# A two-level Strassen-Winograd channel product on one core: second pass in groups of 1024 tokens, with all weights read from DRAM

## The chip, the cores and the metric

The kernel runs on one core of one Trainium2 chip. The metric is device time in microseconds of one execution, measured on the core. Smaller is better. Everything is fp32.

## What is computed

An attention block without softmax is followed by an MLP mixer. B = 8 batches, 8 heads of 64, S = 576 tokens, 512 channels.

```python
kv = np.einsum('bhsd,bhse->bhde', k, v)
out = np.einsum('bhsd,bhde->bhse', q, kv)
rms = np.sqrt(np.mean(out * out, axis=-1, keepdims=True) + 1e-06)
x = (out / rms * g_norm)                 # then heads are put side by side: (B, S, 512)
h = np.maximum(x.transpose(0, 2, 1) @ w_tok1, 0.0) @ w_tok2      # 576 -> 256 -> 576
u = x + h.transpose(0, 2, 1)
h2 = np.maximum(u @ w_ch1, 0.0) @ w_ch2                          # 512 -> 1536 -> 512
return u + h2
```

The change concerns the last two lines, the channel product over all 8 x 576 = 4608 tokens.

## The kernel before

The **first pass** computes attention and the token mixing for pairs of batches, and writes u to DRAM (`u_dram`). It ends at about 197 us of the profiled execution and is not touched.

The tokens are cut into nine units of 512: unit b (0 to 7) holds the first 512 tokens of batch b, unit 8 the 64 last ones of all batches. **Group 0** (unit 0) is computed by `channel1_once` and `channel2_once` with one level of Strassen-Winograd, seven products of half-size matrices in place of eight. Meanwhile the weights for the second pass are prepared: `mix_ch1`, `mix_ch2` make the sums of the outer level, `split` those of the inner level.

The **second pass** computes groups 1 to 8, one unit each, with two levels: `channel1` (u times w_ch1) and `channel2` (times w_ch2) each have seven outer blocks (`ORDER1`, `ORDER2`), and each block has seven inner products of three matmuls with 128 moving columns, both levels numbered 1 to 7. The inner level of one block is the function `outer`. A block starts every seven *places*; `PLACE` says at which place after the start of its block each inner product stands, so that neighbouring blocks interleave. `put(place, step)` hangs other steps (evictions of PSUM, sums on VectorE, transfers) behind the product of a place. At the end of the program one loop walks through the places and emits the product and then the steps; every engine and queue gets its work in this order.

The inner products of a block share PSUM tiles: a takes products 1, 6, 7 and 4 in turn and is read after each; c gets a copy of product 1 and product 2 on top; b takes 5 and 3. Tiles a and b come from a ring of six (`m_psum`), c from a ring of two. Where a block has a `base` (blocks 2, 5 and 4 of channel1, block 6 of channel2) the reads are adds on VectorE, else copies on ScalarE. `write` joins a PSUM tile with what was read before (u2, u3).

Of the seven weight parts of a block, four lie in SBUF (`w_ch1`, `w_ch2`, the outer sums in `late["w2"]`, `d2`); the three inner sums are stored by `split` to DRAM (`sums_dram`) and fetched by `fetch_sums` three blocks ahead. All of `split` runs on VectorE with three buffers (`sv`).

The activations come to `uT`, transposed, by a way of their own: `fetch_t` loads a tile of u, `turn_blocks` transposes 32x32 blocks on VectorE and stores them to DRAM, `fetch_u` reads them in the order wanted. `outer_u` and `inner_u` fill the 7x7 outer and inner sums of `uT`. In channel2 the steps `ins[o]` make the inner sums of the hidden activations, A and S1 to S4 their outer sums, `xadd` and `radd` add the finished blocks to the residual `xg`, and `store` writes the result. Some sums of channel1 run on GpSimd.

All transfers here are issued on SyncE's queue (SP), except the stores of u_dram (GpSimd) and some at the very end (ScalarE).

Of the kernel before, what the change touches and what calls it, by code (L numbers as in the profile page):

```python
# [20 lines left out]
def kernel(  # L21
# [49 lines left out]
    NG = B + 1  # L71
# [8 lines left out]
    consts = pool("consts", 1)  # L80
# [19 lines left out]
    w_ch1 = consts.tile([P, 4, 4, FQ], F32, name="w_ch1")  # L100
    w_ch2 = consts.tile([P, 4, NS, DH], F32, name="w_ch2")
# [3 lines left out]
    u_dram = [dram.tile([J * P, DM], F32, name=f"u_dram{g}") for g in range(NG)]  # L105
# [126 lines left out]
    IN = {1: {5: 0, 6: 1, 3: 2}, 2: {5: 0, 6: 1, 4: 2}}  # L232

    def part(weight, o, n, sums=None):

        if n in IN[weight]:
            t = sums[:, IN[weight][n]]
            return t if weight == 1 else t.rearrange("p (w e) -> p w e", w=W)
        if weight == 1:
            return (w_ch1[:, SA[o]] if SA[o] < 4 else late["w2"][:, SA[o] - 4])[:, SA[n]]  # L240
        return w2_of(o)[:, ts(int(n in (2, 3)), W), ts(int(n in (7, 3)), P)]
# [34 lines left out]
    def w2_of(n):  # L276
# [3 lines left out]
    sums_dram = {(w, o): dram.tile([P, 3, FQ], F32, name=f"sums{w}{o}")  # L280
                 for w in (1, 2) for o in SA}

    def sums_tile():
        return late["sums"].tile([P, 3, FQ], F32, name="sums", tag="sums")

    def split(weight, o):


        at = []
        steps = (s_sums if weight == 1 else t_sums)(lambda n: part(weight, o, n, at[0]))  # L290

        def first():
            at.append(late["sv"].tile([P, 3, FQ], F32, name="sv"))
            steps[0]()

        def last():
            steps[3]()
            dma(sums_dram[weight, o], at[0])

        return [first, steps[1], last], steps[2]  # L300
# [244 lines left out]

    def fetch_x(g, i):

        if g < NG:
            if i == 0:
                xg[g] = late["xg"].tile([P, J, DM], F32, name="xg")  # L550
            dma(xg[g][:, ts(i, 2)], u_dram[g].rearrange("(t p) e -> p t e", p=P)[:, ts(i, 2)])

    def fetch_t(g, i):

        if g < NG:
            xt[g, i] = late["xt" if g else "xt0"].tile([P, DM], F32, name="xt")
            dma(xt[g, i], u_dram[g][ts(i, P)])

# [4 lines left out]
    def turn_blocks(g, i):  # L565
        if g >= NG:
            return
        half, n = i // 2, 2 * (i % 2)
        if n == 0:
            blocks[g] = late["y" if g else "y0"].tile([P, NC, 2, NC, Q], F32, name="y")  # L570
        for o in range(2):
            keep(nc.vector.transpose(
                blocks[g][:, :, o, n:n + 2].rearrange("p b n t -> p n b t"),
                xt[g, i][:, ts(o, DH)].rearrange("p (n b t) -> p n b t", n=2, b=NC)))
        if n:
            t = blocks_dram[g, half] = dram.tile([NC, Q, NC, 2 * P], F32, name=f"blocks{g}{half}")
            for a in range(NC):
                dma(t[:, :, a].rearrange("b i x -> i b x"),
                    blocks[g][ds(a * Q, Q)].rearrange("p b o n t -> p b (o n t)"))

    def fetch_u(g, half):

        if g >= NG:
            return
        if half == 0:
            uT[g] = late["u"].tile([P, 7, NC, 7, Q], F32, name="uT")
        for o in range(2):
            dma(uT[g][:, 2 * half + o, :, :4].rearrange("p a n t -> p a (n t)"),
                blocks_dram[g, half].rearrange("b i a x -> (b i) a x")[:, :, ts(o, P)])

    def outer_u(g):

        return t_sums(lambda n: uT[g][:, SB[n], :, :4]) if g < NG else []

    def inner_u(g, lo, hi):

        return t_sums(lambda n: uT[g][:, lo:hi, :, SB[n]]) if g < NG else []
# [6 lines left out]
    def v_tile(g, i):  # L604

        if (g, i) not in V:
            V[g, i] = late["v"].tile([P, NS, 2, P], F32, name=f"v{i}")
        return V[g, i]
# [11 lines left out]
    def r_tile():  # L620
        return late["r"].tile([P, 2, DH], F32, name="r", tag="r")

    def channel1_once(g):
# [4 lines left out]
        def pair(d):  # L628
# [15 lines left out]
            def first():  # L644
                for n in ("t1", "u2", "u3"):
                    at[n] = r_tile().rearrange("p i (j t) -> p i j t", j=2)
                for n in (1, 6, 7, 5):
                    at[f"p{n}"] = m_psum(shape, f"ps_v{n}")
                product(1, at["p1"], True, False)
                copy(at["t1"], at["p1"])  # L650
# [34 lines left out]
    def channel2_once(g):  # L685
# [16 lines left out]
        t1, u2, u3 = (r_tile() for _ in range(3))  # L702
# [24 lines left out]
        def fourth():  # L727
            product(4, p7, False, True)
            tensor_add(quarter(1, 0), p7, quarter(1, 0))
            store(g, xg, 1)  # L730

        def third():
            product(3, p5, False, True)
            tensor_add(quarter(0, 1), p5, quarter(0, 1))
            store(g, xg, 0)
# [6 lines left out]
    PLACE = {1: 0, 2: 8, 6: 3, 5: 4, 7: 6, 4: 9, 3: 12}  # L742
# [5 lines left out]
    def outer(place, size, mul, to, base=None, act=copy, onto=False):  # L748

        banks, t = {}, {}

        def product(n, name, start, stop):
            if start:
                banks[name] = m_psum([P, size], f"ps_{name}")
            mul(n, banks[name], start, stop)

        def temp(n, bufs):
            t[n] = late["tmp"].tile([P, FQ], F32, name=n, tag=n, bufs=bufs)[:, :size]
            t[n] = fit(t[n])
            return t[n]

        def fit(flat):
            return flat if size == P else flat.rearrange("p (w t) -> p w t", w=W)

        def read(o, i, j):

            if base:
                tensor_add(o, fit(banks["a"]), base(i, j))
            else:
                copy(o, fit(banks["a"]))

        def read_first():
            banks["c"] = late["c"].tile([P, DM], F32, name="ps_c", tag="c")[:, :size]
            read(fit(banks["c"]), 0, 0)

        def write(i, j, name, n):  # L780
            tensor_add(to(i, j), fit(banks[name]), to(i, j) if onto else t[n])

        def put_on(i, j, n):
            if onto:
                tensor_add(to(i, j), to(i, j), t[n])

        def take(i, j, name, act):
            if onto:
                tensor_add(to(i, j), banks[name], to(i, j))
            else:  # L790
                act(to(i, j), fit(banks[name]))

        def at(n, name, start, stop, *steps):
            def all_of():
                product(n, name, start, stop)
                for step in steps:
                    step()

            products[place + PLACE[n]] = all_of

        at(1, "a", True, False, read_first)
        at(6, "a", False, False, lambda: read(temp("u2", 2), 0, 1))
        at(5, "b", True, False)
        at(7, "a", False, False, lambda: read(temp("u3", 1), 1, 1))
        at(2, "c", False, True, lambda: take(0, 0, "c", act))
        put(place + PLACE[7] + (1 if onto else 2), do(put_on, 1, 1, "u3"), do(write, 1, 1, "b", "u3"))
        at(4, "a", False, True, lambda: take(1, 0, "a", copy) if onto else read(to(1, 0), 1, 0))
        put(place + PLACE[4], do(put_on, 0, 1, "u2"))
        at(3, "b", False, True)
        put(place + PLACE[3] + 1, do(write, 0, 1, "b", "u2"))  # L810

# [12 lines left out]
    sums, v_in_parts = {}, {}  # L824

    def fetch_sums(n):
        if n < len(order):
            w, _, o = order[n]
            sums[n] = sums_tile()
            dma(sums[n], sums_dram[w, o])  # L830

# [3 lines left out]
    def channel1(g, n0):  # L837
# [4 lines left out]
        def first(i, o):  # L842
            n = n0 + i

            def mul(p, ps, start, stop):
                for w in range(W):
                    matmul(ps[:, ts(w, P)], lhsT=part(1, o, p, sums[n])[:, ts(w, P)],
                           rhs=uT[g][:, SB[o], :, SB[p]], start=(start and w == 0), stop=stop,
# [3 lines left out]
            outer(7 * n, FQ, mul, lambda i, j: sub(v_tile(g, TO[o]), i, j),  # L852
                  base and (lambda i, j: sub(v_tile(g, base), i, j)), relu if o in (2, 4) else copy)
            put(7 * n + PLACE[3] + 1, do(fetch_sums, n + 3))

        for i, o in enumerate(ORDER1):
            first(i, o)

# [8 lines left out]
        for place, step in zip((21, 22), add(3, 3, 1)):  # L867
            put(b + place, step)
        for place, i, j in ((30, 0, 0), (31, 1, 1), (32, 1, 0), (35, 0, 1)):
            put(b + place, do(lambda i, j: tensor_add(*(sub(v_tile(g, t), i, j) for t in (1, 4, 3)),  # L870
                                                      engine=nc.gpsimd), i, j))
        put(b + 43, *add(7, 5, 4, nc.gpsimd))

        for t, *places in ((2, None, 29, 28, 25), (7, 47, 47, 48, 48), (1, None, 50, 46, 47)):
# [4 lines left out]
        for place, f, i in ((18, turn_blocks, 0), (19, fetch_t, 1), (29, turn_blocks, 1), (30, fetch_t, 2),  # L879
                            (40, turn_blocks, 2), (41, fetch_t, 3), (49, turn_blocks, 3), (70, fetch_t, 4)):  # L880
            put(b + place, do(f, g + 1 + i // J, i % J))
        if g > 1:
            steps = outer_u(g)[1:]
            for place, step in zip((0, 0, 2, 3, 4, 5, 7, 9), steps + [inner_u(g, 1, 2)[2]] + inner_u(g, 2, 7)):
                put(b + place, step)

    def channel2(g, n0):
# [3 lines left out]
        def second(i, o):  # L891
# [3 lines left out]
            def mul(p, ps, start, stop):  # L895
                v = v_in_parts[g, o](p)
                w = part(2, o, p, sums[n])
                for s in range(W):
# [357 lines left out]
```

## Time and profile before

| what | value |
|---|---|
| median of three runs | 806.33 us (806.32 to 810.31) |
| the profiled execution | 805.97 us |
| its span, first to last instruction | 803.9 us |
| first pass ends, group 0 begins (TensorE) | 196.8 us |
| channel2_once begins | 233.7 us |
| first product of the second pass | 264.7 us |
| one group of the second pass | 65.8 us |
| last matmul ends | 798.7 us |

The span is what the profile covers; 2.1 us of the execution lie outside it. A matmul's end is modelled in the profile, so durations of single matmuls overlap, and the rate is read from one start to the next. The stage boundaries are starts of the first matmul on the tiles ps_v, ps_w and ps_a in TensorE's timeline. These are the transfers that the change has to do with, with their number, size and the median time from issue to landing:

```profile
sums<-sums SPq DMA_DIRECT2D x112, 576.0 KB, 4.1
...
xt<-u_dram SPq DMA_DIRECT2D x36, 256.0 KB, 4.1
blocks<-y SPq DMA_DIRECT2D x72, 128.0 KB, 2.6
uT<-blocks SPq DMA_DIRECT2D x36, 256.0 KB, 4.8
...
sums<-sv SPq DMA_DIRECT2D x14, 576.0 KB, 2.8
```

### The profile page before, as it was taken

How to read it: one execution, taken by the hardware profiler on the slowest of the kernel's cores; microseconds unless marked ns; L12 is line 12 of the kernel's file. 1: busy time of each engine (PE TensorE's matmuls, PEld its weight loads, DVE VectorE, ACT ScalarE, POOL GpSimd, SP SyncE). 2: the span in 40 equal slices, each digit the busy share in tenths (PEclk: the TensorE clock that was granted, in tenths of full speed). 3: DMA queues.
4: the chain of work that ended last, by engine and by line, in shares of the span. 5: the costliest groups of instructions: out<-in, count | busy, mean ns of one | idle time of the engine just before them, and what ended most of it. 6: DMA issues, size and time to landing. Idle time of an engine off the chain costs nothing.

```text
span 803.9 us, 17541 instructions
## 1 busy us (share of the span) xinstructions
PE 784.7 (98%) x7008; PEld 692.2 (86%) x7008; DVE 645.0 (80%) x1265; ACT 294.3 (37%) x761; POOL 91.3 (11%) x93
## 2 busy tenths in 40 slices
PE   5999999999999999999999999999999999999997
PEld 5655545535888999999999999999999999999997
DVE  2666576796896978978987987997897899799687
ACT  2356564845210224234244234333423423423331
POOL 1211111111000021011003003001101200300300
PEclk9999999999999999999999999999999999999999
DMA  9999998457258477378468648738736845864642
GB/s 291 310 337 333 350 360 297 158 188 243 102 182 287 176 229 231 129 221 269 155 194 249 198 148 259 220 117 274 254 123 221 262 160 189 245 199 134 208 148 82
DMA packets 95040, 175.49 MB, mean 218 GB/s; under 512 B 7024, under 2 KB 54128, under 8 KB 94960
## 3 DMA queue, kind: packets, MB, share of 16 engines
q1 hardware_dynamic: 90656, 163.21, 63.3%
q0 software_dynamic: 2624, 9.44, 3.0%
q10 hardware_dynamic: 1680, 1.74, 0.7%
q8 instruction: 55, 0.90, 0.4%
q14 instruction: 25, 0.20, 0.1%
HBM read 137.79 MB, written 36.57 MB: 217 GB/s over the span
## 4 chain that ended last, share of the span: by engine, by line
PE 89%; DMA 4%; DVE 3%; ACT 2%; issue 1%; SPq 0%; ACTq 0%; DVEq 0%
PE ps_a L128 37%; PE ps_b L128 19%; PE ps_c L128 10%; PE ps_h L128 8%; PE ps_u L128 7%; PE ps_v L128 3%; PE ps_kv L128 2%; DMA v_in<-in_v_dram 2%; PE ps_w L128 2%; PE ps_o L128 2%; ACT x L453 1%; DMA k_in<-in_k_dram 1%; DMA sums<-sums 1%; DVE uT L119 1%; DVE sv L119 1%
## 5 line engine op out<-in xcount | busy, mean ns | idle before, releaser
L119 POOL TENSOR_TENSOR v<-v,v 128x384 f32<-128x384 f32 (+1 forms) x48 | 61.4, 1300 | 504.4 <-ACT v L125 464.6
L125 ACT COPY u<-ps_a 128x128 f32<-128x128 f32 (+1 forms) x160 | 56.1, 351 | 157.8 <-PE ps_a L128 155.7
L128 PE MATMUL ps_b<-uT,sums 128*128 128x128 f32 x672 | 86.3, 276 | 0.2 <-DVE v L119 0.2
L128 PEld LDWEIGHTS ps_b<-uT,sums 128*128 128x128 f32 x672 | 80.7, 192 | 0.5 <-DVE v L119 0.4
L119 DVE TENSOR_TENSOR v<-v,v 128x768 f32<-128x768 f32 (+1 forms) x86 | 79.4, 931 | 1.5 <-ACT r L125 0.5
L128 PE MATMUL ps_a<-uT,w_ch 128*128 128x128 f32 x576 | 78.8, 275 | 0.0
L125 ACT COPY ps_c<-ps_a 128x128 f32<-128x128 f32 (+1 forms) x80 | 26.9, 336 | 129.6 <-PE ps_a L128 97.9
L119 DVE TENSOR_TENSOR v<-ps_b,u 128x384 f32<-128x384 f32 x112 | 61.4, 548 | 13.7 <-PE ps_b L128 12.0
L128 PEld LDWEIGHTS ps_a<-uT,w_ch 128*128 128x128 f32 x576 | 71.5, 192 | 0.1
L128 PE MATMUL ps_u<-h,w_tok 128*128 128x512 f32 (+1 forms) x160 | 67.3, 607 | 0.2
L128 PE MATMUL ps_h<-x,w_tok 128*128 128x512 f32 (+1 forms) x160 | 65.4, 603 | 0.0
L119 DVE TENSOR_TENSOR uT<-uT 128x512 f32<-128x512 f32 (+4 forms) x103 | 63.0, 628 | 0.8
L128 PE MATMUL ps_a<-uT,w 128*128 128x128 f32 x432 | 60.0, 275 | 0.0
L128 PEld LDWEIGHTS ps_a<-uT,w 128*128 128x128 f32 x432 | 54.0, 192 | 0.0
L128 PEld LDWEIGHTS ps_h<-x,w_tok 128*128 128x128 f32 (+1 forms) x160 | 26.1, 189 | 31.9 <-issue 27.7
L128 PEld LDWEIGHTS ps_u<-h,w_tok 128*128 128x128 f32 (+1 forms) x160 | 24.7, 179 | 31.2 <-issue 25.4
L119 DVE TENSOR_TENSOR xg<-xg,r 128x512 f32<-128x512 f32 x74 | 49.9, 684 | 0.7
L119 DVE TENSOR_TENSOR sv<-v 128x384 f32<-128x384 f32 x80 | 43.3, 550 | 8.8 <-ACT v L122 8.8
L122 ACT ACTIVATE v<-v 128x384 f32<-128x384 f32 (+1 forms) x86 | 42.5, 528 | 21.4 <-DVE v L119 20.9
L399 DVE TENSOR_TENSOR x<-ps_o,g_sb 128x512 f32<-128x512 f32 x32 | 21.5, 686 | 34.6 <-PE ps_o L128 30.0
L128 PE MATMUL ps_a<-uT,sums 128*128 128x128 f32 x336 | 46.9, 276 | 1.2 <-DMA sums<-sums 1.0
L128 PE MATMUL ps_a<-sums,sv 128*128 128x128 f32 x336 | 47.0, 276 | 0.0
(131 smaller groups left out, 1560.1 us busy)
## 6 DMA issues: line engine op xcount, KB each, us to landing
sums<-sums SPq DMA_DIRECT2D x112, 576.0 KB, 4.1
qT<-in_q_dram SPq DMA_DIRECT2D x8, 1152.0 KB, 9.1
xt<-u_dram SPq DMA_DIRECT2D x36, 256.0 KB, 4.1
blocks<-y SPq DMA_DIRECT2D x72, 128.0 KB, 2.6
uT<-blocks SPq DMA_DIRECT2D x36, 256.0 KB, 4.8
xg<-u_dram SPq DMA_DIRECT2D x18, 512.0 KB, 5.3
k_in<-in_k_dram SPq DMA_DIRECT2D x16, 512.0 KB, 9.0
u_dram<-x POOLq DMA_DIRECT2D x16, 512.0 KB, 6.3
```

What stands on the lines that cost most here:

```text
L119: keep(engine.tensor_tensor(out=o, in0=a, in1=b, op=op))
L122: keep(nc.scalar.activation(o, a, AF.Relu))
L125: keep(nc.scalar.copy(o, a))
L128: keep(nc.tensor.matmul(*a, **kw))
L399: keep(nc.vector.tensor_mul(x, bank[c, h], g_sb.to_broadcast([P, number(c), D])))
L453: keep(nc.scalar.activation(x[:, k, h], x[:, k, h], AF.Copy, scale=inv[:, k, h]))
```

## The change

Groups 1 to 4 of the second pass now hold two units each (`units`), so 1024 tokens. channel1's matmuls have 256 moving columns (T), and there are half as many of them. In channel2 the moving side is the weights, 128 columns as before; its matmuls are as many as before, two row tiles to a product. Sums, evictions and residual adds are half as many and twice as long.

None of the weights stays in SBUF after group 0. `split` stores all seven parts of a block to DRAM: three (of the block itself) as they are, two sums made on VectorE and two on GpSimd. It has two buffers for w_ch1 (during channel1_once) and one for w_ch2 (`svb`, during channel2_once and the first twelve places). `fetch_w` reads the parts in four pieces, into two buffers each, at 12, 9, 7 and 4 places before their block.

PSUM is cut anew: a and b have one tile of two banks each, d has two. a takes products 1 and 2; d gets a copy of product 1 and then 6, 7 and 4; b takes 5 and 3. The places within a block change with it. The last block of all has an order of its own (`LAST`).

The inner sums of the activations are no longer kept for all of `uT`; `inner_u` makes four for each block, two buffers ahead, and the outer sums lie in a ring of three (`us`). The transposition of the two units of the next group is spread over channel1. In the change-over from group 0, unit 2 is transposed and fetched during channel2_once.

```diff
-    NG = B + 1
+    NU = B + 1
+    NG = 1 + B // 2
+    T = 2 * P
...
+        def first():
+            at.append(late["sv0"].tile([P, 4, FQ], F32, name="sv0"))
+            for n in (1, 2, 4 if weight == 1 else 3):
+                dma(wide(to[:, POS[n]]), of(n))
+            if weight == 1:
+                tensor_add(own(5), of(7), of(4))
+            else:
+                tensor_add(own(5), of(7), of(1), ALU.subtract)
+
+        def second():
+            tensor_add(own(6), own(5), of(1), ALU.subtract) if weight == 1 else tensor_add(
+                own(6), of(3), own(5), ALU.subtract)
+
+        def third():
+            tensor_add(own(7), of(1 if weight == 1 else 3), of(7), ALU.subtract, nc.gpsimd)
+
+        def fourth():
+            tensor_add(own(3 if weight == 1 else 4), of(2), own(6), ALU.subtract, nc.gpsimd)
...
+                dma(to[:, 1:3], t[:, :2])
+                dma(to[:, 5:], t[:, 2:])
...
-    PLACE = {1: 0, 2: 8, 6: 3, 5: 4, 7: 6, 4: 9, 3: 12}
+    PLACE = {1: 0, 5: 1, 6: 3, 2: 4, 3: 5, 7: 6, 4: 9}
+    LAST = {1: 0, 5: 1, 6: 3, 2: 4, 7: 5, 3: 6, 4: 7}
...
+        def first():
+            bank("a")
+            mul(1, banks["a"], True, False)
+            bank("d")
+            copy(banks["d"], banks["a"])
+
+        def fifth():
+            bank("b")
+            mul(5, banks["b"], True, False)
+            read(temp("p5", 2), "b", 1, 1)
...
+        def sixth():
+            mul(6, banks["d"], False, False)
+            read(temp("u2", 1), "d", 0, 1)
...
+        def join(i, j, name, n):
+            tensor_add(to(i, j), fit(banks[name]), to(i, j) if onto else fit(t[n]))
...
+        put(place + places[3], do(join, 0, 1, "b", "u2"))
+        put(place + places[7], do(join, 1, 1, "d", "p5"))
...
+    def fetch_ahead(n):
+        for k, place in enumerate((-12, -9, -7, -4)):
+            if 7 * n + place >= 0:
+                put(7 * n + place, do(fetch_w, n, k))
...
             def mul(p, ps, start, stop):
+                wt, u = w_part(n, p), u_part(g, o, p)
                 for w in range(W):
-                    matmul(ps[:, ts(w, P)], lhsT=part(1, o, p, sums[n])[:, ts(w, P)],
-                           rhs=uT[g][:, SB[o], :, SB[p]], start=(start and w == 0), stop=stop,
+                    matmul(ps[:, ts(w, T)], lhsT=wt[:, ts(w, P)],
+                           rhs=u.rearrange("p a n t -> p n a t"), start=(start and w != 1), stop=stop,
...
+            for place, step in zip((-4, -2, 2, 5), inner_u(g, o)):
...
-        for place, step in zip((21, 22), add(3, 3, 1)):
+        for place, step in zip((15, 18), add(3, 3, 1)):
...
+        for k, place in enumerate((12, 17, 23, 27, 33, 37, 42, 46)):
+            u = units(g + 1)[k // J]
+            put(b + place, do(turn_blocks, u, k % J))
...
+        for place, step in zip((-2, 1, 10, 18), outer_u(g)):
...
+    late["sv0"] = pool("svb", 1, "right", w2s)
+    fill, turns = lasts + parts2[:20], turn_unit(2)
+    for i, f in enumerate(turns):
+        fill.insert(3 * i, f)
...
+    fill += [do(fetch_u, 1, 1, 0), do(fetch_u, 1, 1, 1), do(fetch_w, 1, 1)] + inner_u(1, 1)[:2] + outer_u(1)[:1]
+    weave(channel2_once(0), fill)
+    banks.close()
+    for n, size in (("a", 1), ("b", 1), ("d", 2)):
+        late[n] = pool(n, size, space=bass.MemoryType.PSUM)
...
+    for n, f in enumerate(parts2[20:]):
+        put(2 + 3 * n // 2, f)
```

## The prediction

> **What bounds the kernel now.** I read the page first, then TensorE's waits, the stretches of the second pass, and the order of time on single engines. TensorE has work almost throughout, and the chain of work that ended last is made of it:
>
> ```profile
> span 803.9 us, 17541 instructions
> PE 784.7 (98%) x7008; PEld 692.2 (86%) x7008; DVE 645.0 (80%) x1265; ACT 294.3 (37%) x761; POOL 91.3 (11%) x93
> ...
> PE 89%; DMA 4%; DVE 3%; ACT 2%; issue 1%; SPq 0%; ACTq 0%; DVEq 0%
> ```
>
> The waits of TensorE, longest first, are small, and only these lie in the part that changes:
>
> ```profile
> PE ps_a L128 <- DMA sums<-sums: 1.0, 1, 1.0
> ...
> PE ps_a L128 <- ACT ps_c L125: 0.2, 1, 0.2
> ...
> PE ps_b L128 <- DVE v L119: 0.2, 1, 0.2
> ```
>
> So TensorE's own rate and new waits are what count. Its rate is read from starts in the timeline, since ends are modelled:
>
> ```profile
> 209.49 1.89 PE L128 MATMUL ps_v<-uT,w_ch 128*128 128x256 f32 x8
> 211.21 1.89 PE L128 MATMUL ps_v<-uT,w 128*128 128x256 f32 x8
> 212.94 1.89 PE L128 MATMUL ps_v<-uT,w_ch 128*128 128x256 f32 x8
> ```
> ```profile
> 277.42 0.83 PE L128 MATMUL ps_a<-uT,w 128*128 128x128 f32 x6
> 278.09 0.83 PE L128 MATMUL ps_a<-uT,w_ch 128*128 128x128 f32 x6
> 278.76 0.83 PE L128 MATMUL ps_c<-uT,w 128*128 128x128 f32 x6
> ```
>
> An fp32 matmul leaves two records. Eight records of 256 columns take 1.727 us, so one matmul 432 ns; six of 128 columns take 0.670 us, so one 223.4 ns. Two narrow ones (446.8) against one wide one save 15.0 ns. Next, how full VectorE is. The columns are length, then busy time (and count) of TensorE, weight load, VectorE, ScalarE, GpSimd, then clock, DMA share, GB/s; the first line is one group of 512 tokens, the second a busy stretch of the first-group code:
>
> ```profile
> 303.60:369.40 65.80, 65.80 (x590) 65.78 (x590) 56.87 (x117) 22.86 (x65) 7.68 (x6) 1.00 0.65 207
> 245.00:255.00 10.00, 10.00 (x48) 8.81 (x47) 6.22 (x12) 0.00 (x0) 0.00 (x0) 1.00 1.06 379
> ```
>
> VectorE is at 86% and stalls nobody. Back to back it takes less than its mean duration, 0.465 us for 384 elements where the group's mean is 0.55:
>
> ```profile
> 275.09 0.55 DVE L119 TENSOR_TENSOR v<-ps_b,u 128x384 f32<-128x384 f32 x1
> 275.56 0.55 DVE L119 TENSOR_TENSOR w_ch<-w_ch 128x384 f32<-128x384 f32 x1
> 276.02 0.55 DVE L119 TENSOR_TENSOR d<-d 128x384 f32<-128x384 f32 x1
> ```
>
> The same 0.08 taken off other means gives steps of 0.34 (256 elements), 0.60 (512), 0.87 (768), 1.68 (1536).
>
> [...]
>
> **The change, part by part.**
>
> *Wide products.* channel1 has 7x7x3 = 147 matmuls for each of 8 groups, 1176; they become 588. 588 x 15.0 ns = 8.8 us less on the path. channel2 keeps 128 columns and the same number of matmuls. A place of the order takes 3 x 0.432 = 1.30 us in channel1 and 6 x 0.2234 = 1.34 in channel2 (before: 0.67).
>
> *VectorE in total.* A group of 1024 tokens has, in channel1: 14 joins and 12 adds of 768 (22.6), 28 `inner_u` of 256 (9.4), 4 `outer_u` of 1024 (4.6), 2 adds of 1536 (3.4), 8 pairs of transposes of 0.76 (6.1) = 46; in channel2: 28 sums of 768 (24.4), 10 of 1536 (16.8), 10 of 1024 (11.4), 18 of 256 (6.0) = 59. 105 of 129 us is 81%, less than the 86% now. VectorE doesn't become the bound on average.
>
> *PSUM in groups.* Before, b lay in a ring of six and a join could be late by several products. Now a and b have one buffer each. The join of product 3 (place 5) must have read b before product 5 of the next block (place 8): two products, 2.6 us. d is equally short. So VectorE may lag by about 2.6 us, and its work is bunched. Counting lag place by place (work at the steps above, less 1.30 per place): it is level at the end of product 15; p5 (0.87) and the 1536 add (1.68) leave 2.55; place 16 (one `ui`, 0.34) leaves 1.6; place 17 (u2 0.87, `ui` 0.34, transposes 0.76) 2.3; place 18 (a read of a 0.87, the other 1536 add 1.68, `outer_u` 1.14) 4.7; the join of place 19 is finished at 4.7 - 1.3 + 0.87 = 4.2 us after its product, against 2.6: late by 1.6, the join of d behind it by 1.9 in all. At places 37 to 41, where `ins[1]` adds four sums of 0.87 to the reads of block 4, the same count gives 1.3. That is 3.2 a group, 1.6 in the last (no transposes): 11 us. Bounds: 0, if VectorE is ahead when it arrives, and 16, if waits between dependent adds (0.58 instead of 0.47 in the timeline) are added. The same count for the kernel before gives a largest lag of 1.8, which its ring of six absorbs. I take 9.
>
> *Weights from DRAM.* Seven parts of each of the 14 blocks are stored, 14 x 7 x 196.6 KB = 19.3 MB where 8.3 were. Read: 4 x 19.3 = 77 MB against 66. Each fetch stands 12 places, 16 us, ahead of its use, and lands in 4.1 (row of sums). Steady traffic is near 30 MB in 129 us, 230 GB/s: hidden. A part that is late costs directly; I take nothing, at most 0.5 us a block (28 in all).
>
> *Change-over.* Here the cover goes. In channel2_once (7 products of 5.18 us, 36.3) five `split(2, o)` are woven in, with one buffer `svb`. Each first add on VectorE waits for the stores of the split before it. One round: two adds 1.0, two GpSimd adds 2 x 1.0 (its 128x384 row), issue 0.3, landing 2.8 (row sums<-sv), 6.1 at least; with four transposed-block stores (0.43 each to issue) ahead on SP and VectorE's other work I get starts at 13, 22, 30, 37.5 and 44 us. VectorE takes its work in order, so behind the waiting fifth split stand the last read of PSUM (0.6) and the two first `ui` sums that place 1 needs (46 us, where TensorE is ready at 37.6). And `fetch_u` of unit 2 stands on SP behind the last store of that split, which waits for two GpSimd adds, and behind `store(0, 0)`, which waits for VectorE: issued at 48 us, four of them, landed at 53 (4.8 by the row uT<-blocks), then two `outer_u` sums of 1.14, one add of a split and `ui` 7: 56. TensorE would reach the product that needs it (place 6) at 36.3 + 5 x 1.30 = 42.8. Wait 13.3 us, part of it already at place 1. Bounds: 4 (rounds of 5.7, from 13) and 22 (traffic here is 14 MB, at 379 GB/s 38 us, more than the 36.3 available, and landing then takes the 9 of the loads of k_in). The trace of before loses 1.2 at this spot (the 1.0 and 0.2), which goes. In channel1_once the splits have two buffers and GpSimd takes half; one more transposition ahead of the first reads of PSUM: +1.
>
> *End.* In the last block seven products stand in eight places without a gap to work off the sums: VectorE has 10.6 us behind place 43 where TensorE has 8; I get its last add 3 us after TensorE's ideal end, 0.9 now. Stores similar. +2.5 (1 to 4).
>
> Sum: 803.9 - 8.8 + 9 + 13.3 - 1.2 + 1 + 2.5 = 819.7 of span. Outside the span lie 805.97 - 803.9 = 2.1; the median of the runs is 0.4 above the profiled execution. 822.
>
> **Rivals.** (1) Only the change-over costs, since TensorE's own pauses put VectorE ahead: 822 - 9 = 813. For it: 81% against 86%; against it: the single b. (2) The other side: landing in the change-over is fast enough that place 6 is met within about 4 us, and VectorE stalls are below 1 and the end costs 1: 803.9 - 8.8 - 1.2 + 4 + 1 + 1 + 2.1 = 802. It decides when a split round is below 5.7 us. [...] (3) Weights arrive late: 0.5 us a block, 822 + 28 = 850, if SP is held up by waits for VectorE (its longest now are 12.6 and 19.2 us); against it: 16 us of lead.
>
> **How the numbers follow.** Forecast 0.50 (own range 814 to 830), rival 1 0.17, rival 2 0.26, of which half is faster and half within 0.5%, rival 3 0.07. A difference under 0.5% (4 us) can't be told from none. Faster 0.13, same 0.15, slower 0.72. Range 802 to 834.
>
> **What would show it.** Right: 128x256 matmuls at 432 ns; a pause of TensorE of 10 us or more, in pieces, just after channel2_once with VectorE or uT as releaser; in each group short waits of ps_b or ps_d for VectorE near a third and four fifths of channel1. Wrong: no gap at the change-over, or waits for w parts.

## The result and the profile after

The changed kernel takes 868.49 us (median of four runs, 866.68 to 869.07), the kernel before 806.33; the ratio is 1.0755, with a 95% interval of 1.0724 to 1.0787. The profiled execution of the changed kernel has a span of 864.9 us where the one before had 803.9, so 61.0 us are to be explained. The direction was forecast, the size was not: 822 us, with a range up to 834.

These lines of the page of the changed kernel answer to the first ones shown of before:

```profile
span 864.9 us, 14846 instructions
PE 793.9 (92%) x5832; PEld 656.8 (76%) x5832; DVE 641.7 (74%) x890; ACT 265.3 (31%) x513; POOL 118.6 (14%) x97
...
PE 50%; DVE 16%; DMA 7%; issue 3%; SPq 2%; POOL 1%; ACT 0%; DVEq 0%; POOLq 0%; ACTq 0%
```

TensorE's share of the chain that ended last fell from 89% to 50%, VectorE's rose from 3% to 16%, although VectorE is busy for a smaller share of the span than before (74% against 80%). That is the pattern of an engine that has capacity but is late at certain places. TensorE's waits say which (engine, tile and line; releaser; sum, times, longest one):

```profile
PE ps_d L131 <- DVE v L122: 13.9, 9, 2.6
PE ps_b L131 <- DVE ui L122: 12.0, 1, 12.0
PE ps_d L131 <- DVE u L122: 9.0, 4, 2.5
...
PE ps_b L131 <- DVE v L122: 6.2, 6, 1.7
PE ps_b L131 <- DVE sv L122: 3.9, 4, 1.0
...
PE ps_d L131 <- DVE ui L122: 3.0, 1, 3.0
...
PE ps_d L131 <- DVE xg L122: 2.7, 1, 2.7
```

The two with `ui` are the change-over, once each. The others with `v`, `u` and `sv` come back in each of the four groups, and `xg` is the end. No wait of TensorE for a weight `w` stands in this list. Nor does anything wait for GpSimd's sums in channel1: in the list of the waits of all engines GpSimd is the releaser once, for 0.2 us, in the first pass, and the queue SP waits for it only ahead of stores of `sv`, the sums of the splits. So it is not the slowness of these sums themselves that delays the work behind them.

The change-over in TensorE's timeline (start, duration; the bracket is idle time before the instruction and its releaser):

```profile
270.10 1.46 PE L131 MATMUL ps_a<-uT,w 128*128 128x256 f32 x6
283.58 2.93 PE L131 MATMUL ps_b<-ui,w 128*128 128x256 f32 x6 [12.03 <-DVE ui L122]
286.30 2.76 PE L131 MATMUL ps_d<-ui,w 128*128 128x256 f32 x6
288.86 1.85 PE L131 MATMUL ps_a<-uT,w 128*128 128x256 f32 x6
290.55 1.46 PE L131 MATMUL ps_b<-uT,w 128*128 128x256 f32 x6
295.04 1.32 PE L131 MATMUL ps_d<-ui,w 128*128 128x256 f32 x5 [3.03 <-DVE ui L122]
```

Starts are 1.30 us apart when TensorE runs freely. After the pause of 12.03 us two steps of 2.72 and 2.56 us follow: TensorE came back at half its clock (0.50 from 283.6 to 288.8 us). The table of stretches (columns as before: length, busy time of TensorE, weight load, VectorE, ScalarE and GpSimd, then clock, DMA share, GB/s) shows how full the DMA engines are while channel2_once runs, in the kernel before (first line) and in the changed one (second line); its last line shows the slow clock of the changed kernel:

```profile
234.00:270.00 36.00, 36.00 (x172) 31.76 (x171) 29.39 (x48) 0.59 (x1) 0.00 (x0) 1.00 0.63 223
...
234.00:270.00 36.00, 36.00 (x168) 31.69 (x168) 21.25 (x35) 1.22 (x2) 9.14 (x8) 1.00 0.97 309
...
283.60:288.80 5.20, 5.20 (x12) 4.13 (x13) 0.38 (x1) 0.80 (x1) 0.58 (x1) 0.50 1.01 332
```

What the forecast did not have at all is seen when the timelines of GpSimd and VectorE in group 2 are laid side by side:

```profile
471.70 1.82 POOL L122 TENSOR_TENSOR v<-v,v 128x768 f32<-128x768 f32 x1 [1.23 <-DVE v L122]
...
478.26 3.47 POOL L122 TENSOR_TENSOR v<-v,v 128x1536 f32<-128x1536 f32 x1 [2.30 <-DVE v L122]
487.04 3.54 POOL L122 TENSOR_TENSOR v<-v,v 128x1536 f32<-128x1536 f32 x1 [5.31 <-DVE v L122]
...
472.23 0.91 DVE L122 TENSOR_TENSOR p<-ps_b,v 128x768 f32<-128x768 f32 x1
...
478.03 3.98 DVE L122 TENSOR_TENSOR ui<-us,ui 128x256 f32<-128x256 f32 x2
...
486.88 0.41 DVE L122 TENSOR_TENSOR ui<-us 128x256 f32<-128x256 f32 x1
...
487.90 3.51 DVE L122 TENSOR_TENSOR sv<-v 128x768 f32<-128x768 f32 x1
```

An add on VectorE of 256 elements takes 0.41 us (at 486.88, begun just before GpSimd's sum at 487.04). Two of them take 3.98 us at 478.03, while GpSimd adds 1536 elements: the first began before GpSimd and took 0.42 us, the second ended 0.3 us after GpSimd. At 487.90 an add of 768 elements takes 3.51 us beside another GpSimd sum. At 472.23 an add of 768 elements with one input in PSUM takes its usual 0.91 beside a GpSimd sum. All overlaps from 268 us on say the same. Of 30 VectorE adds with both inputs in SBUF that began while GpSimd was adding, 29 were drawn out (the other one began 0.07 us before GpSimd's end). Of 13 that began before GpSimd none was, and of 15 adds with an input in PSUM none was. The rows by shape (count, busy time, mean ns) give the sum of it; the first three are VectorE's, the last two GpSimd's:

```profile
L122 DVE TENSOR_TENSOR sv<-v 128x768 f32<-128x768 f32 x40 | 48.6, 1222 | 0.0
L122 DVE TENSOR_TENSOR ui<-us,ui 128x256 f32<-128x256 f32 x24 | 29.0, 1222 | 0.0
L122 DVE TENSOR_TENSOR sv<-v,sv 128x768 f32<-128x768 f32 x28 | 26.6, 949 | 0.0
...
L122 POOL TENSOR_TENSOR v<-v,v 128x768 f32<-128x768 f32 x16 | 29.6, 1861 | 381.6 <-ACT v L128 376.7 <-DVE v L122 4.9
L122 POOL TENSOR_TENSOR v<-v,v 128x1536 f32<-128x1536 f32 x8 | 28.1, 3509 | 27.3 <-DVE v L122 27.3
```

Two adds of the same size, `sv<-v` and `sv<-v,sv`, have the same mean when undisturbed (948 and 951 ns in e1_memset below); here the first has 1222 ns, the second 949. `ui<-us,ui` has 1222 ns where an undisturbed one has some 416.

A ledger of the 61.0 us. A pause is the time from one start of TensorE to the next above the ideal step (1.295 or 1.340 us a product), steps of over 0.12 us only:

| stage | before | after |
|---|---|---|
| pauses in the change-over (waits 12.03 and 3.03, the slow clock 3.1) | 1.5 | 18.5 |
| pauses in the four groups (eight before) | 0.3 | 46.8 |
| pause at the end | none | 2.9 |
| start of the last product to the end of the span | 6.0 | 9.4 |
| wide products in place of narrow ones | 0 | -8.8 |

That is 17.0 + 46.5 + 2.9 + 3.4 - 8.8 = 61.0. The expectations below that name sums of pauses have those of the groups 2 to 3 us too small; under "Measured" they are all counted as here. One group takes 141.6 us (from 456.80 to 598.38, the same product of groups 2 and 3), where two groups of before took 131.6.

### The profile page after: what moved, and what is told of

Its sections match the earlier page's. It is cut to its first block, busy times and chain, and to the rows that moved or that the text cites. A ratio compares the mean times of both kernels' runs of the same rounds, so it can differ in the third digit from the quotient of the medians.

```text
span 864.9 us, 14846 instructions
## 1 busy us (share of the span) xinstructions
PE 793.9 (92%) x5832; PEld 656.8 (76%) x5832; DVE 641.7 (74%) x890; ACT 265.3 (31%) x513; POOL 118.6 (14%) x97
## 4 chain that ended last, share of the span: by engine, by line
PE 50%; DVE 16%; DMA 7%; issue 3%; SPq 2%; POOL 1%; ACT 0%; DVEq 0%; POOLq 0%; ACTq 0%
PE ps_d L131 22%; PE ps_b L131 14%; PE ps_a L131 13%; DVE v L122 4%; DVE sv L122 4%; DMA xt<-u_dram 4%; DVE ui L122 3%; SPq L119 2%; DVE y L590 1%; DMA parts<-sv 1%; DVE u L122 1%; DVE xg L122 1%; POOL sv L122 1%; PE ps_u L131 1%; DVE us L122 1%
## 5 line engine op out<-in xcount | busy, mean ns | idle before, releaser
L131 PE MATMUL ps_d<-ui,w 128*128 128x256 f32 x504 | 124.8, 393 | 25.9 <-DVE v L122 13.9
L131 PEld LDWEIGHTS ps_d<-ui,w 128*128 128x128 f32 x504 | 96.0, 195 | 46.2 <-DVE v L122 19.4
L131 PE MATMUL ps_b<-w,sv 128*128 128x128 f32 x672 | 84.9, 276 | 3.9 <-DVE sv L122 3.9
L131 PE MATMUL ps_a<-w,v 128*128 128x128 f32 x672 | 84.2, 275 | 0.0
L131 PEld LDWEIGHTS ps_b<-w,sv 128*128 128x128 f32 x672 | 79.5, 192 | 4.8 <-DVE sv L122 4.7
L131 PEld LDWEIGHTS ps_a<-w,v 128*128 128x128 f32 x672 | 79.8, 192 | 0.2
L122 DVE TENSOR_TENSOR v<-v,v 128x1536 f32<-128x1536 f32 (+1 forms) x46 | 74.4, 1624 | 0.3
L131 PE MATMUL ps_d<-w,v 128*128 128x128 f32 x528 | 66.9, 277 | 2.7 <-DVE xg L122 2.7
L131 PEld LDWEIGHTS ps_d<-w,v 128*128 128x128 f32 x528 | 63.3, 193 | 3.0 <-DVE xg L122 2.9
L131 PE MATMUL ps_d<-w,sv 128*128 128x128 f32 x480 | 60.1, 275 | 0.0
L131 PEld LDWEIGHTS ps_b<-ui,w 128*128 128x128 f32 x168 | 32.4, 196 | 25.4 <-DVE ui L122 12.4
L122 DVE TENSOR_TENSOR sv<-v 128x768 f32<-128x768 f32 x40 | 48.6, 1222 | 0.0
```

The costliest lines, as they stand in the source:

```text
L122: keep(engine.tensor_tensor(out=o, in0=a, in1=b, op=op))
L131: keep(nc.tensor.matmul(*a, **kw))
```

## The experiments

The theory for the groups: VectorE stands still in an add with two SBUF inputs while GpSimd reads SBUF (T1). The main rival: VectorE is simply full (T2). For the change-over the theory was at first the single buffer of the splits, as forecast.

**e1_memset.** In place of the GpSimd sums of channel1, GpSimd writes zeros.

```diff
-            put(b + place, do(lambda i, j: tensor_add(*(sub(v_tile(g, t), i, j) for t in (1, 4, 3)),
-                                                      engine=nc.gpsimd), i, j))
-        for place, step in zip((36, 39), add(7, 5, 4, nc.gpsimd)):
-            put(b + place, step)
+            put(b + place, do(lambda i, j: keep(nc.gpsimd.memset(sub(v_tile(g, 1), i, j), 0.0)), i, j))
+        for i, place in enumerate((36, 39)):
+            put(b + place, do(lambda i: keep(nc.gpsimd.memset(half(v_tile(g, 7), i), 0.0)), i))
```

> The GpSimd sums of channel1 (four of 768 and two of 1536 elements in each group) are left out: in their place GpSimd writes zeros into the same tiles, so it reads no SBUF there. Theory T1 (an add on VectorE with both inputs in SBUF stands still while GpSimd reads SBUF): the stretched adds go, ui sums stay at or below 0.5 us and sv<-v of 768 at about 0.95, the wait of ps_d at place 19 (about 2 us a group) and the change-over remain; 831 us, give or take 5. Rival T2 (VectorE is simply full, GpSimd has nothing to do with it): nothing changes but the few waits for GpSimd itself, 860 to 868. Rival T3 (any instruction on GpSimd stretches VectorE, one that only writes too): ui sums of over 1 us still stand beside the GpSimd writes, over 845.

Measured: 840.57 us, 28 us less than the changed kernel. The rows by shape:

```profile
L122 DVE TENSOR_TENSOR sv<-v 128x768 f32<-128x768 f32 x40 | 37.6, 948 | 0.0
...
L122 DVE TENSOR_TENSOR ui<-us,ui 128x256 f32<-128x256 f32 x24 | 9.7, 416 | 0.0
```

Every drawn-out add in the groups is gone: in these two rows 11.0 and 19.3 us of VectorE's time. (Five remain from the change-over up to 304 us, beside GpSimd's sums of the splits.) The pauses in the groups fall from 46.8 to 19.0 us, those of the change-over (19.8) and the end (2.9) stay. T2 falls: VectorE has the same adds to do and TensorE pauses 27.8 us less. The total is 5 us above the stated band, since the pauses that remained in the groups were larger than assumed. Against T3 there are few readings, since the writes mostly come where VectorE does little in SBUF. Four adds with two SBUF inputs begin while GpSimd writes, one in each group, and take 0.38 to 0.42 us; GpSimd's write and one of them:

```profile
458.48 2.70 POOL L957 MEMSET v<- 128x1536 f32 x2
...
458.61 0.38 DVE L122 TENSOR_TENSOR ui<-us 128x256 f32<-128x256 f32 x1
```

**e2_copy.** The same sums are replaced by GpSimd copies of one input.

```diff
-                                                      engine=nc.gpsimd), i, j))
-        for place, step in zip((36, 39), add(7, 5, 4, nc.gpsimd)):
+            put(b + place, do(lambda i, j: keep(nc.gpsimd.tensor_copy(sub(v_tile(g, 1), i, j), sub(v_tile(g, 4), i, j))), i, j))
+        for i, place in enumerate((36, 39)):
...
+            put(b + place, do(lambda i: keep(nc.gpsimd.tensor_copy(half(v_tile(g, 7), i), half(v_tile(g, 5), i))), i))
```

> The same GpSimd sums are left out, and GpSimd copies one of their inputs to the same tile instead: it reads SBUF, with one input. T1 (reading is what stops VectorE): ui and sv<-v adds beside a copy are stretched to about the copy's end; 840 to 866 by how long the copies are. T1' (only a GpSimd instruction with two inputs from SBUF stops VectorE): no stretch, about 831 as with the zeros. T2: 860 to 868.

Measured: 847.20 us, pauses in the groups 25.9. GpSimd's copies are short (1.53 and 1.60 us for 1536 elements), and so is the harm. A copy and the adds beside it in the timelines of group 2:

```profile
474.13 1.53 POOL L957 COPY v<-v 128x1536 f32<-128x1536 f32 x1 [3.29 <-DVE v L122]
...
473.91 2.02 DVE L122 TENSOR_TENSOR ui<-us,ui 128x256 f32<-128x256 f32 x2
```

Two adds that take 0.75 us when undisturbed take 2.02 and end within 0.3 us of the copy. Of the adds with two SBUF inputs, all 12 that began while GpSimd copied were drawn out, and none of the 12 that began before the copy. So one input that GpSimd reads from SBUF is enough, and the harm grows with the length of the GpSimd instruction. T1' falls.

**e3_sums_on_vector.** The six sums go to VectorE at the same places; the edit is `engine=nc.vector` for `engine=nc.gpsimd` in the two lines.

> The six GpSimd sums of channel1 go to VectorE at the same places, nothing is left out. T1: some 8.5 us of stretched VectorE time a group go, 4 x 0.87 + 2 x 1.68 = 6.8 come; the total stays within 15 us of the changed kernel, 853 to 868, and no ui sum is above 0.6 us. T2 (VectorE full, GpSimd harmless): VectorE gets 6.8 us a group more with nothing in return, 870 to 895.

Measured: 855.11 us, in the lower half of T1's band. The kernel is 13 us faster although VectorE has more to do: undisturbed, `ui<-us,ui` has a mean of 417 ns. The pauses in the groups are 31.4: 15.4 saved against the changed kernel, 12.4 given back against e1_memset for adds at crowded places.

**e4_changeover.** The splits of w_ch2 get two half tiles in place of one, all their sums on VectorE, and `fetch_u` of unit 2 comes earlier.

```diff
+                at.append(late["sv0"].tile([P, 2, FQ], F32, name="sv0", tag="sv0"))
...
+            if weight == 2:
+                dma(to[:, 1:3], at[0])
...
+                at.append(late["sv0"].tile([P, 2, FQ], F32, name="sv1", tag="sv1"))
...
-                dma(to[:, 1:3], t[:, :2])
-                dma(to[:, 5:], t[:, 2:])
+                dma(to[:, 5:], at[1])
...
+    fill[36:36] = [do(fetch_u, 1, 1, 0), do(fetch_u, 1, 1, 1)]
```

> Only the change-over is altered: the splits of w_ch2 use two half tiles, all their sums are on VectorE, each half is stored as soon as it is made, and the activations of unit 2 are fetched ahead of the first stores of group 0. Theory C (the single buffer of the splits, with its round of sums, store and wait, and the fetch of unit 2 behind it make the pauses of 12.0 and 3.0 us): both pauses shrink to 5 us or less in all, with them the drop of TensorE's clock at 281 to 289 us goes; 853 to 857, and the groups lose the same as before. Rival (memory traffic or VectorE's total work bounds the change-over, not the order): the pauses stay above 10 us, 864 to 870.

Measured: 863.13 us. The pauses of the change-over went from 18.5 only to 14.2 us (waits of 10.6 and 1.3). Theory C is for the most part wrong: with the round of sums, store and wait taken apart most of the pause is still there. The table of stretches has the DMA engines nearly as full as before the edit:

```profile
234.00:270.00 36.00, 36.00 (x169) 31.69 (x168) 21.45 (x40) 1.22 (x2) 2.00 (x2) 1.00 0.95 303
```

From here on the rivals were the issue time of SP (Q), the bytes (M), and the order of the work on VectorE (R), each tried on top of e4_changeover.

**e7_scalar_queue.** In `first` of the first five splits of w_ch2 the three stores of raw parts go to ScalarE's queue:

```diff
-                dma(wide(to[:, POS[n]]), of(n))
+                dma(wide(to[:, POS[n]]), of(n), nc.scalar if weight == 2 and o in ORDER2[:5] else nc.sync)
```

> Starts from e4_changeover (863.1 us, pauses of 10.6 and 1.3 us left). The 15 stores of raw parts of w_ch2 in the first five splits (0.2 MB each) are issued on ScalarE's queue and no longer on SP. Theory Q (SP's issue time, 0.6 to 0.7 us each and about nine tenths of the time from 234 to 283 us, is what makes the change-over late): SP gets some 9.8 us free, the pauses shrink to 4 us or less, 852 to 856. Theory M (the DMA engines themselves are full, share 0.97 at 308 GB/s in that stretch): the same bytes must still move, the pauses stay at 9 us or more, 860 to 865.

Measured: 862.66 us, pauses of 16.0 us (4.8 of them now ahead of the second pass, at a product of channel2_once). Q falls.

**e8_raw_later.** The same 15 stores are collected in a list `raws` and come after the change-over.

```diff
+    for n, f in enumerate(raws):
+        put(9 + n, f)
...
-    put(16, turn_over)
-    put(22, do(fetch_x, 1, 0))
-    put(26, do(fetch_x, 1, 1))
+    put(24, turn_over)
+    put(28, do(fetch_x, 1, 0))
+    put(32, do(fetch_x, 1, 1))
```

> Starts from e4_changeover. The same 15 stores stay on SP but are issued at places 9 to 23 of group 1, after the change-over; turn_over and the fetches of x move to places 24, 28 and 32 for it. Nothing is left out. Theory M: 2.95 MB fewer in the change-over, at 305 GB/s 9.7 us less, the pauses shrink from 11.9 to 2 to 4 us; 852 to 856, if the transfers of group 1 take the extra bytes without being late. Theory Q: the same here, and in e7_scalar_queue too. Theory R (neither: VectorE's own order and the chain from load to transposition to store to fetch set the time, by latency): both e7 and e8 keep pauses of 9 us or more.

Measured: 863.36 us. The pause is 8.0 us, 10.5 with the slow clock, where M had 2 to 4. M alone was not enough, and the DMA engines were no longer full; this is the table of stretches for this kernel:

```profile
234.00:270.00 36.00, 36.00 (x168) 31.73 (x167) 22.41 (x41) 1.22 (x2) 1.99 (x2) 1.00 0.84 264
```

VectorE stood idle for 3.0, 1.2, 4.8 and 2.5 us ahead of the four transpositions of unit 2, each time for the tile `xt`. What the change-over won was lost again in group 1, where the stores now ran (waits of 1.2, 2.1 and 4.7 us there).

**e9_chain.** On top of e8_raw_later the work woven into channel2_once is put in another order: each `fetch_t` directly behind the transposition before it.

```diff
-    fill, turns = lasts + parts2[:20], turn_unit(2)
-    for i, f in enumerate(turns):
-        fill.insert(3 * i, f)
...
+    fill += [do(turn_blocks, 2, 0), do(fetch_t, 2, 1)] + parts2[:2] + [do(fetch_w, 0, 0)] + parts2[2:4]
+    fill += [do(turn_blocks, 2, 1), do(fetch_t, 2, 2)] + parts2[4:6] + [do(fetch_w, 0, 1)] + parts2[6:8]
...
```

> Starts from e8_raw_later (863.4 us; DMA share 0.84 up to 270 us, yet a pause of 8.0 us left, 10.5 with the slow clock behind it). Only the order of the work woven into channel2_once is altered: each fetch of a tile of unit 2 stands directly behind the transposition of the tile before, four to six steps ahead of its own transposition, where one or two splits stood between. Theory R (what is left of the pause is VectorE standing in order at a transposition whose tile was fetched too late: 3.0, 1.2, 4.8 and 2.5 us of idle time for xt in e8): the pause of place 1 shrinks to 2 us or less; 853 to 857. If the bytes still decide (13.5 MB up to 283 us): the pause stays at 7 us or more, 861 to 864.

Measured: 858.74 us, a pause of 4.1 us, 7.2 with the slow clock. The idle times for `xt` are 1.3 us or less. The pause is above R's 2 us, and the DMA engines are nearly full again, at 0.96.

**e11_chain_alone.** The order of e9_chain on top of e4_changeover; the raw stores stay in the change-over.

> Starts from e4_changeover (863.1 us, pauses of 10.6 and 1.3 us) with only the order of e9_chain in the work of channel2_once; the 15 raw stores stay in the change-over. If bytes and order both bound the change-over (the rival to a single cause): DMA share stays at 0.95 or more, the pauses stay at 8 us or more, 860 to 863. If the order alone was the cause and e8's move of the stores was of no use: pauses of 4 to 6 us, 856 to 859, as e9_chain.

Measured: 859.64 us, pauses of 11.2 us with the slow clock, at a full DMA:

```profile
234.00:270.00 36.00, 36.00 (x169) 31.69 (x168) 22.74 (x42) 1.22 (x2) 2.00 (x2) 1.00 1.00 319
```

So both count. From the 14.2 us of e4_changeover the moved bytes alone take 3.7, the order alone 3.0, both together 7.0. What the other 7.2 us come from was not tested further.

**e5_sums_moved.** On top of the changed kernel, its change-over left alone: the GpSimd sums go to VectorE, and crowded places are thinned out.

```diff
-        for place, step in zip((15, 18), add(3, 3, 1)):
+        for place, step in zip((15, 21), add(3, 3, 1)):
...
-        for place, step in zip((36, 39), add(7, 5, 4, nc.gpsimd)):
+        for place, step in zip((49, 50), add(7, 5, 4)):
...
-                (-12, [ins[1][0]]), (-11, [ins[1][2]]), (-10, [ins[1][1]]), (-8, [ins[1][3]]),
+                (-6, [ins[1][0]]), (-4, [ins[1][1]]), (-2, [ins[1][2]]), (-1, [ins[1][3]]),
```

> The six GpSimd sums of channel1 go to VectorE and are spread over the places: in each group add(3,3,1) moves to places 15 and 21, the last outer_u to 22, ins[1] to places -6, -4, -2, -1, ins[4][0] to 13, the sums for block 7 to 49 and 50. Nothing is left out; the change-over is that of the changed kernel. If contention with GpSimd and the bunching of VectorE's work in a few places are the whole loss of the groups, then the waits of ps_b and ps_d for VectorE inside the groups nearly go: the kernel with the GpSimd sums left out had 39 us of pauses in all from the change-over on, of them 16 in the groups, so 840.6 - 16 = 824, give or take 4. If VectorE is simply too full for the sums (81% by count before, 6.8 us a group more), the lag comes back elsewhere: 845 or more, as with the sums on VectorE at the old places (855.1).

Measured: 835.63 us, 33 us less than the changed kernel, with the whole work done. It misses the 824 of the first theory and beats the 845 of the second. The pauses in the groups are 13.2; most of them come from one wait in the list of TensorE's waits:

```profile
PE ps_b L131 <- DVE sv L122: 7.4, 8, 1.0
```

It came four times in the changed kernel, once a group, and comes eight times here, twice a group. The second one is of my making: I had moved `ins[4][0]` from place 6 to 13, too late for the product of place 15.

**e10_all** puts e9_chain, e5_sums_moved and two more moves in channel2 together. The moved stores and `turn_over` stand three places earlier than in e9_chain.

```diff
-                (8, [A[0]]), (9, [A[1]]), (10, [ins[2][3]]), (11, [S3[0]]), (12, [S3[1]]),
-                (13, [ins[4][1]]), (14, [ins[4][2]]), (15, [S2[0]]),
+                (8, [A[0]]), (9, [A[1]]), (10, [ins[2][3]]), (11, [ins[4][0]]), (12, [S3[0], ins[4][1]]),
+                (14, [ins[4][2]]), (15, [S3[1], S2[0]]),
...
-                (31, [ins[5][0], ins[6][3]])
+                (30, [ins[6][3]]), (31, [ins[5][0]])
```

> All repairs together: e9_chain, the sums of e5_sums_moved on VectorE, and in channel2 ins[4][0] at place 11 and ins[6][3] at place 30, each ahead of the long sums that delayed it (two waits of ps_b for sv, about 1 us each a group). Nothing is left out. Without any pause this kernel would take about 800.5 us (832.7 of span in e5_sums_moved less its 34.3 of pauses, plus 2.1). With an end of 2.9, a change-over of 2 to 6 and 0.5 to 1 a group: 808 to 813, the same as the kernel before or up to 0.9% slower. If the wide product's 8.8 us were not a gain at all, it would stay above 815.

Measured: 821.99 us, 1.0189 of the kernel before (1.0172 to 1.0207). So it is slower, not the same, and outside the 808 to 813 that were expected. Pauses: 5.7 in the change-over, 15.5 in the groups, of these 9.7 in group 1, 2.9 at the end. A later group takes 132.0 us where two of before took 131.6: its pauses of 2.5 us use up the 2.2 us that the wide products save in it.

**e12_all** moves the fetches of x of group 1 from places 28 and 32 to 40 and 46, and two sums of xg behind the last joins.

> Starts from e10_all (822.0 us, of its 21.1 us of pauses 7.2 from the change-over, 9 in group 1, 2.9 at the end, 3 elsewhere). The fetches of x for group 1 move from places 28 and 32 to 40 and 46, behind those of the tiles to be transposed, for which VectorE waited 2.5 us twice; at the end two sums of xg (1.2 us each) are put behind the last joins, so that PSUM tile d is read earlier. If these two waits were the cause: one of the pauses of group 1 (3.2 us and the slow clock behind it) goes, and the end loses 1 to 2 us: 814 to 819, still slower than the kernel before. If group 1 is late because of the bytes of the moved stores: 820 to 823.

Measured: 821.78 us, ratio 1.0179 (1.0157 to 1.02), no change. The end lost 1.1 us of its pause and the wait of 3.2 us in group 1 shrank to 0.9, but two others there grew (1.9 to 2.8, and a new 1.9). This fits the second of the two cases, that group 1 is late because of the transfers that the moved stores put there: VectorE stands idle there for tiles `xt`, 3.4, 1.2 and 2.9 us the longest. And e9_chain, which has these stores in group 1, pauses 15.6 us in that group, where e11_chain_alone pauses 12.0. No run with all the repairs does without the moved stores. No version here beats the kernel before.

## Why the prediction was wrong

*Wide products: right.* 588 x 15.0 ns = 8.8 us was a rate, and the rate holds: a product, six records of three matmuls, takes 1.295 us.

*Weights from DRAM: right.* 12 places of lead were enough: the pieces of `w` landed in 3.6 and 3.2 us (medians), and no wait for `w` came.

*VectorE in total and PSUM in groups: here the forecast failed.* The count took each add at its undisturbed step, 0.34 us for 256 elements and 0.87 for 768, and gave 3.2 us a group. Its 1.14 for 1024 elements was an estimate for a shape that the trace of before lacks; it lies on the line between 0.87 (768) and 1.68 (1536), and it holds: in the changed kernel adds of 1024 elements start 1.13 and 1.14 us apart. At the place where the bunching was forecast it was right: place 19, late by 1.6 and 1.9 in all, measured 1.82 and 0.24 in group 2; for places 37 to 41 the count had 1.3, and e1_memset has 0.77 + 0.43 + 0.24 = 1.44 there. It missed the wait for `sv` in channel2, 1.15 us a group. With the GpSimd sums left out the pauses are 19.0 us over four groups, where I took 9 and gave 16 as the upper bound, so this term alone was also too small. The term that was missing is the other 27.8 us. The sums on GpSimd were left out of VectorE's load and then costed at nothing, when they still held VectorE up. They did no harm in the second pass before. Of the VectorE adds beside them there, 65 had an input in PSUM, and the 8 with both inputs in SBUF had all begun before GpSimd; none was drawn out, and the adds `sv` kept one mean:

```profile
L119 DVE TENSOR_TENSOR sv<-v 128x384 f32<-128x384 f32 x80 | 43.3, 550 | 8.8 <-ACT v L122 8.8
```

But the trace of before had such an add in the first pass, GpSimd's and VectorE's lines:

```profile
80.04 2.78 POOL L461 TENSOR_TENSOR x<-x,inv 128x512 f32<-128x512 f32 x2 [1.91 <-DVE inv L439]
...
81.83 1.54 DVE L457 TENSOR_TENSOR x<-x,inv 128x512 f32<-128x512 f32 x1
83.77 0.68 DVE L457 TENSOR_TENSOR x<-x,inv 128x512 f32<-128x512 f32 x1
```

The same instruction takes 1.54 us when it begins beside GpSimd and 0.68 alone. I had read over it. What the runs show of it: of the adds with two SBUF inputs 29 of 30 were drawn out that began while GpSimd was adding, all 12 that began while it copied, and none of the 13 and 12 that began first; that a write is harmless rests on four overlaps (0.38 to 0.42 us). Why the two engines get in each other's way was not shown. The change makes this worse in two ways: GpSimd's sums are twice as long (3.5 us for 1536 elements, 1.9 for 768 before), and the inner sums `ui`, two SBUF inputs each, now stand among them. That b and d are too short to absorb such delays, as the prediction had it for bunched work, fits the waits of ps_b and ps_d, but no run here gives the changed kernel longer rings.

*Change-over: nearly right in size, half wrong in cause.* Forecast 13.3 us of waiting, measured 15.1; split starts forecast at 13, 22, 30, 37.5 and 44 us, measured at 14.5, 24.4, 31.3, 40.3 and 46.5 after the start of channel2_once. But e4_changeover takes the round of the single buffer away and wins 4.3 of 18.5 us. Half of the rest (7.0 of 14.2) was what the prediction had only as its upper bound, 14 MB in 36.3 us, together with the order in which VectorE stood at the transpositions; the other half stays open. The 379 GB/s of that bound, from 10 us of the kernel before (share 1.06), was too high: in the change-over the DMA engines were full at 303 to 319 (share 0.95 to 1.00 over 36 us). The slow clock after the pause, 3.1 us, was not in the sum.

*End: too small.* Forecast +2.5 with a bound of 4; the pause is 2.9, and the stretch from the last product to the end is 3.4 longer, so 6.3. The lag of VectorE was near the count (2.7 us of wait for `xg` ahead of the last product); the slow clock of the last product (0.50 from 856.3 us on; it lasted 2.31 us where one shortly before lasted 1.50) and the stores queued behind it, 4.3 us of issue on SP, were not in it.

*Rivals.* Rival 3, late weights, came nearest in time (850) for a reason that did not happen. None of the cases had adds of VectorE held up by GpSimd, so none of the chances given covered what happened.

## What to carry to other kernels

A sum moved to another engine is free only if it doesn't hold up the first one: before costing GpSimd at nothing, look at which VectorE instructions run beside it and whether both their inputs lie in SBUF, and compare rows of the same shape, since a mean of 1222 beside 949 ns is a sign of it. Where a buffer ring is made shorter, count on such delays reaching TensorE: here they did, as waits of up to 2.6 us. For a change-over add up the bytes and divide by the rate that a full stretch of that kind of transfer shows (here 303 to 319 GB/s), before counting rounds.

## What the runs showed of the hardware

An add of VectorE with two SBUF inputs that began while a GpSimd instruction with an SBUF input ran was held until about the end of that one, in 29 of 30 cases beside sums and all 12 beside copies: 3.98 us for two adds that take 0.75, beside a GpSimd sum of 3.47; 2.02 beside a copy of 1.53. An add that began before GpSimd was not held (none of 13 in the changed kernel, none of 12 in e2_copy), nor were the 15 adds with an input in PSUM (0.91 us for 768 elements beside a sum).

TensorE ran at half its clock after the long pause: 2.72 and 2.56 us a step where 1.30 is usual, for about 5 us after a pause of 12 us (clock 0.50). It fell after shorter pauses too, but not each time: after a wait of 2.59 us in group 2 two products took 4.38 us where 2.59 is usual (clock 0.61), after an equal wait of 2.58 in group 3 they took 2.69 (clock 1.00).

The 16 DMA engines were full at 303 to 319 GB/s in the change-over (share 0.95 to 1.00), with packets of 1.1 KB on average (11.11 MB in 10269 packets from 234 to 270 us).
